# An attention-then-experts kernel: PSUM banks in another order, tokens transposed one pass ahead, r and k in one transfer

## The chip, the cores and the metric

The kernel runs on one core of a Trainium2 chip. The core has four compute engines with a queue of instructions each: TensorE (PE in the profile; its weight loads are shown as PEld), VectorE (DVE), ScalarE (ACT) and GpSimd (POOL). SyncE (SP) only starts DMA transfers here; POOL starts the indirect ones. Each engine works through its queue in the order of the program, and an instruction that waits holds up everything queued behind it. The metric is the device time of one execution in microseconds.

## The reference

Two blocks follow each other. The first is a linear attention with a decaying state, per batch `b` and head `h`:

```python
for t in range(S):
    cur = u[None] * k_t (outer) v_t
    y[:, :, t] = r_t @ (state + cur)
    state = w * state + k_t (outer) v_t
```

with 4 batches, 8 heads, 768 steps and head size 48. Its output, laid out as 3072 tokens of 384 numbers, goes into a mixture of 8 experts with one expert per token:

```python
logits = x @ w_gate                      # (3072, 8)
e = argmax(logits);  g = softmax(logits)[e]
out[token] = g * (relu(x @ w1[e]) @ w2[e])   # 384 -> 1024 -> 384
```

All inputs and outputs are float32.

## The kernel before

**Attention.** The 32 pairs of batch and head are worked off as 16 units of two heads (`U = 16`, four units per batch), one head in partitions 0 to 47, the other in 64 to 111. A unit is cut into `G = 6` chunks of 128 steps. Within a chunk the attention is a masked 128 x 128 score matrix; between chunks a 48 x 48 state is carried by a scan. The powers of the decay are put into r and k beforehand.

`load(i)` starts three transfers of unit `i` on SP: r and k of the first head into `rks`, r and k of the second head, and v and k in another layout into `vks`. `prep(i)` has three products: `RK`, r and k times the tables of decay (DVE, line 214), `rp`, r times k (POOL, line 217), and `Kd`, the keys with decay for the state (POOL, line 218). Then `p_own` multiplies `rp` by u on TensorE (line 227, the first TensorE work of a unit), `own_t` transposes that on DVE, `p_scores` makes the scores (line 239), `diag` writes u's diagonal on ACT (line 245), `mask` puts the scores above it (DVE), `p_ds` and `scan` make the states, `p_out` the output (lines 282 and 287), `p_tr` and `keep` turn it into token rows `xb` and add up the gate's logits. The loop over `i` is a pipeline written out by hand: unit `i` is scored, unit `i - 1` is put out, unit `i - 2` is transposed, unit `i + 1` is prepared, unit `i + 3` is loaded.

After every fourth unit `choose`, `p_rank` and `slots` find each token's expert and its place in it, and `send` scatters the token rows from `xb` to `rows` in DRAM by an indirect DMA on POOL (line 357), two chunks of 128 tokens in each of three units (three in each of two units for the third batch). `ids` (line 364), a POOL iota, writes the token numbers into `xb` for the next batch but one; it has to wait until the sends that read this `xb` are done. `clear` zeroes a part of `rows` (one large transfer, after unit 3). The weights of the first two experts are loaded in the same loop: `weights(0, 0)` and `weights(0, 1)` after units 6 and 9, expert 1's after units 13 and 14.

**Experts.** A pass is a stretch of an expert's tokens. Expert 0 has two passes (256 tokens, which stand before the last batch is routed, and 160), experts 1 to 6 one of 416 (`CAP`), the last expert two (160 and 256): ten passes. Per pass:

- `load` reads the token rows back into `xs` (four transfers, SP line 386);
- `xT` transposes them on DVE in three instructions (line 395);
- `L1` makes `hT`: for each of 8 groups `f` three matmuls into a bank of `hbank` (line 403), then a relu on ACT (line 405);
- `L2` makes the output: for each of 3 groups `m` eight matmuls into a bank of `ybank` (line 412), then a transpose on DVE (`yq`, line 414);
- `put` multiplies by the gate on DVE (`yo`, line 452) and scatters 32-token groups to the output with up to 13 indirect DMAs on POOL (line 455).

The last pass does its second layer the other way round, with tokens as the rows (`tokens_out`, lines 435 to 440), which leaves two scatters at the end. `xs` has three buffers, `xT`, `hT`, `yq` and `yo` two, the weights three.

The banks are two lists of PSUM tiles. `X23` and `yps` are each one tile of two banks:

```python
hbank = [X01[0], X01[1], X23[:, 0, :], X23[:, 1, :]]     # group f uses hbank[f % 4]
ybank = [yps[:, 0, :], yps[:, 1, :], dsb]                # group m uses ybank[m]
```

The order of the main loop is `xT(k)`, `L1(k)`, `L2(k-1)`, `load(k+1)`, `put(k-1)`, `weights`. TensorE therefore runs L1 of a pass, then L2 of the pass before it; on DVE `xT(k+1)` stands behind the three transposes of `L2(k-1)` and behind `put(k-1)`.

**The beginning.** SP's first transfers are, in order, the decay table `wt`, unit 0, `ubs` (u), unit 1, `wgs` (the gate's weights), unit 2. POOL builds an identity, masks and small tables of numbers (lines 107 to 135), the table `dec` for the scan (162, 163) and `sel`, the matrix by which `p_tr` transposes and multiplies by the gate at once (167, 168; the last of these instructions reads `wgs`). Only then comes `prep(0)`.

Behind the straight path stands a general one (`general`) for inputs that don't fit its bounds; with these inputs it is branched over.

Of the kernel before, what the change touches and what calls it, by code (L numbers as in the profile page):

```python
# [19 lines left out]
DM = H * D  # L20
# [20 lines left out]
def straight(tc, rk, vk, w, ub, wg, w1, w2, out, flag):  # L41
# [24 lines left out]
    hbank = [X01[0].rearrange("p a b -> p (a b)"), X01[1].rearrange("p a b -> p (a b)"), X23[:, 0, :], X23[:, 1, :]]  # L66
    ybank = [yps[:, 0, :], yps[:, 1, :], dsb]


    wt = cp.tile([KP, HP], FP32, name="wt")  # L70
    nc.sync.dma_start(wt, w)
    ubs = cp.tile([KP, HP, 2], FP32, name="ubs")
    wgs = cp.tile([KP, 2, HP, E], FP32, name="wgs")
# [7 lines left out]
    vks = [ca.tile([128, G, 2, 2 * D], FP32, name=f"vk{i}") for i in range(4)]  # L81

    def load(i):
        if i >= U:
            return
        b, hp = divmod(i, HP)
        n0 = 64 if i < 3 else D
        nc.sync.dma_start(rks[i % 3][0:n0], rk[b, hp, 0, 0:n0])
        nc.sync.dma_start(rks[i % 3][64:KP], rk[b, hp, 1, 0:D])
        nc.sync.dma_start(vks[i % 4], vk[b, hp])  # L90

    load(0)
    nc.sync.dma_start(ubs, ub)
    load(1)
    nc.sync.dma_start(wgs, wg)
    load(2)
# [10 lines left out]
    ident = cp.tile([128, 128], FP32, name="ident")  # L107
    make_identity(nc, ident)
# [4 lines left out]
    tri = cp.tile([128, 128], BF16, name="tri")  # L113
    ones = cp.tile([128, 128], BF16, name="ones")
    nc.gpsimd.tensor_copy(tri, strict)
    nc.gpsimd.memset(ones, 1.0)
    rev = cp.tile([128, E], FP32, name="rev")
    basef = cp.tile([128, E], FP32, name="basef")
    osum = cp.tile([128, E], BF16, name="osum")
    pos = cp.tile([128, CAP // 32], FP32, name="pos")  # L120
    pos2 = cp.tile([128, 4], FP32, name="pos2")
    it = cp.tile([128, 64], I32, name="it")
    nc.gpsimd.iota(it[:, 0:E], pattern=[[-1, E]], base=E, channel_multiplier=0)
    nc.gpsimd.tensor_copy(rev, it[:, 0:E])
    nc.gpsimd.iota(it[:, E:2 * E], pattern=[[N // 128, E]], base=0, channel_multiplier=0)
    nc.gpsimd.tensor_copy(osum, it[:, E:2 * E])
    nc.gpsimd.iota(it[:, 2 * E:3 * E], pattern=[[N, E]], base=0, channel_multiplier=0)
    nc.gpsimd.tensor_copy(basef, it[:, 2 * E:3 * E])
    ng = CAP // 32
    for a in range(4):  # L130
        q = slice(32 * a, 32 * a + 32)
        nc.gpsimd.iota(it[q, 32:32 + ng], pattern=[[32, ng]], base=0, channel_multiplier=1)
    nc.gpsimd.tensor_copy(pos, it[:, 32:32 + ng])
    nc.gpsimd.iota(it[:, 48:52], pattern=[[128, 4]], base=0, channel_multiplier=1)
    nc.gpsimd.tensor_copy(pos2, it[:, 48:52])

# [18 lines left out]
    for hp in range(HP):  # L155
        nc.tensor.transpose(tr[:, hp * 128:hp * 128 + KP], T3c[:, hp, :], ident[0:KP, 0:KP])
    T3 = cp.tile([128, HP, 2 * D], FP32, name="T3")
    nc.scalar.copy(T3.rearrange("p a (h d) -> p a h d", h=2),
                   tr.rearrange("p (a h d) -> p a h d", a=HP, h=2)[:, :, :, 0:D])

    dec = cp.tile([KP, HP, D, G - 1], FP32, name="dec")
    nc.gpsimd.memset(dec, 0.0)
    nc.gpsimd.tensor_copy(dec[:, :, :, 1:], bc(pw[:, 7, :, None, None], [KP, HP, D, G - 2]))
    for par in range(2):
        for h in range(2):
            o = 64 * (h ^ par)
            nc.gpsimd.tensor_copy(sel[:, par, :, h * D:(h + 1) * D], bc(ident[0:KP, None, o:o + D], [KP, HP, D]))
    nc.gpsimd.tensor_copy(sel[:, :, :, 2 * D:], wgs)
# [3 lines left out]
    nc.vector.tensor_scalar(out=le, in0=wt, scalar1=W_HI, scalar2=None, op0=ALU.is_le)  # L172
    nc.vector.scalar_tensor_tensor(out=okw, in0=wt, scalar=W_LO, in1=le, op0=ALU.is_ge, op1=ALU.mult)
# [35 lines left out]
    def prep(i):  # L209
        if i >= U:  # L210
            return
        hp = i % HP
        x, v = rks[i % 3], vks[i % 4]
        nc.vector.tensor_tensor(RKs[i % 3][0:KP].rearrange("p u (c t) -> p u c t", t=C),  # L214
                                x[0:KP].rearrange("p u (c t) -> p u c t", t=C),
                                bc(TT[:, hp, :, None, :], [KP, 2, G, C]), op=ALU.mult)
        nc.gpsimd.tensor_tensor(rps[i % 2][0:KP], x[0:KP, 0], x[0:KP, 1], op=ALU.mult)  # L217
        nc.gpsimd.tensor_tensor(Kds[i % 2], v[:, 0:G - 1, 1, :], bc(T3[:, hp, None, :], [128, G - 1, 2 * D]),  # L218
                                op=ALU.mult)
# [37 lines left out]
    def p_ds(i):  # L257
        v = vks[i % 4]
        d = dsb[:, 0:240].rearrange("p (e g) -> p e g", g=G - 1)
        for c in range(G - 1):  # L260
            for h in range(2):
                nc.tensor.matmul(d[64 * h:64 * h + D, :, c], lhsT=Kds[i % 2][:, c, h * D:(h + 1) * D],  # L262
                                 rhs=v[:, c, 0, h * D:(h + 1) * D], start=True, stop=True, skip_group_check=True)
# [7 lines left out]
    def p_out(i):  # L271
# [8 lines left out]
        for c in range(G):  # L280
            for h in range(2):
                nc.tensor.matmul(o(c, h), lhsT=v[:, c, 0, h * D:(h + 1) * D], rhs=A[:, place(c, h), :],  # L282
# [95 lines left out]
    class Pass:  # L378
# [28 lines left out]
        def L2(self, ms=range(DT)):  # L407
            y = self.y = yqs[self.k % len(yqs)]
            for m in ms:
                p = ybank[m]  # L410
                for f in range(FT):
                    nc.tensor.matmul(p[:, 0:self.n], lhsT=w2s[self.e % 3][:, f, m * 128:(m + 1) * 128],  # L412
                                     rhs=self.h[:, f, 0:self.n], start=f == 0, stop=f == FT - 1, skip_group_check=True)
                nc.vector.transpose(y[:, 0:self.g, 32 * m:32 * m + 32],  # L414
                                    p[:, 0:self.n].rearrange("p (g j) -> p g j", j=32))

        def load_ids(self):

            nt = self.n // 128
            nc.sync.dma_start(xg[:, 0:nt], rows[self.e * N + self.s0:self.e * N + self.s0 + self.n, 2 * D:Q].rearrange(  # L420
                "(t p) c -> p t c", p=128))

        def tokens_out(self):

            nt = self.n // 128
            nc.vector.tensor_scalar(out=vt[:, 0:nt], in0=pos2[:, 0:nt], scalar1=float(self.s0), scalar2=cnt[:, self.e:self.e + 1],
                                    op0=ALU.add, op1=ALU.is_lt)
            nc.vector.memset(it2, 1 << 20)
            nc.vector.tensor_scalar(out=ia[:, 0:nt], in0=xg[:, 0:nt, 1].bitcast(I32), scalar1=2, scalar2=None,
                                    op0=ALU.logical_shift_right)  # L430
            nc.vector.copy_predicated(it2[:, 0:nt], vt[:, 0:nt], ia[:, 0:nt])
            for t in range(nt):
                p = ybank[t]
                for f in range(FT):
                    nc.tensor.matmul(p[:, 0:DM], lhsT=self.h[:, f, t * 128:(t + 1) * 128], rhs=w2s[self.e % 3][:, f, :],  # L435
# [10 lines left out]
        def put(self):  # L446
            yo, ix, g = yos[self.k % len(yos)], ixs[self.k % 2], self.g
# [6 lines left out]
            for k in range(g):  # L454
# [7 lines left out]
    passes = [Pass(0, 0, EARLY, 0), Pass(0, EARLY, CAP - EARLY, 1)] + [Pass(e, 0, CAP, e + 1) for e in range(1, E - 1)] + \  # L462
             [Pass(E - 1, 0, LAST, E), Pass(E - 1, LAST, CAP - LAST, E + 1)]
# [3 lines left out]
    prep(0)  # L467
    for i in range(U + 1):
# [3 lines left out]
        if not last:  # L472
            p_own(i)
            own_t(i)
# [4 lines left out]
        prep(i + 1)  # L479
        if not last:  # L480
# [27 lines left out]
        if i == 3:  # L508
            clear()
        if i in (6, 9):  # L510
            weights(0, (i - 6) // 3)
        if i in (13, 14):
            weights(1, i - 13)
        if i == 14:
            count(cnt3)
            nc.vector.tensor_scalar(out=viol[:, 12:13], in0=cnt3[:, 0:1], scalar1=float(EARLY), scalar2=None, op0=ALU.is_lt)
        if i == U - 1:
            first.load()
    first.xT()
# [39 lines left out]
    first.L2()  # L559
    passes[1].xT()  # L560
    first.put()
    passes[1].L1()
    n = len(passes)
    for k in range(2, n):
        p = passes[k]
        if k == n - 1:
            passes[k - 1].L2()
            passes[k - 1].put()
        p.xT()
        p.L1()  # L570
        if k < n - 1:
            passes[k - 1].L2()
        if k + 1 < n:
            passes[k + 1].load()
        if k < n - 1:
            passes[k - 1].put()
            if 1 < p.e + 2 < E and p.e > 0:
                weights(p.e + 2)
# [10 lines left out]
def general(tc, rk, vk, w, ub, wg, w1, w2, out):  # L589
# [24 lines left out]
    nc.sync.dma_start(wu[0:D], w[0:D])  # L614
    nc.sync.dma_start(wu[64:KP], w[64:KP])
    wgs = consts.tile([128, HP, E], FP32, name="wgsg")
    nc.vector.memset(wgs, 0.0)
    nc.sync.dma_start(wgs[0:KP], wg[:, 0])
# [22 lines left out]
    nc.sync.dma_start(ubg[0:KP], ub)  # L641
# [65 lines left out]
    def load_pair(b, hp):  # L707
# [7 lines left out]
        nc.sync.dma_start(vt, vk[b, hp][:, :, 0, :])  # L715
# [320 lines left out]
def rwkv5_then_switch(tc, rk, vk, w, ub, wg, w1, w2, out):  # L1036
    nc = tc.nc
    with tc.tile_pool(name="fl", bufs=1) as fl:
        flag = fl.tile([1, 1], I32, name="flag")
        with tc.manual_schedule():  # L1040
            straight(tc, rk, vk, w, ub, wg, w1, w2, out, flag)
            bad = nc.values_load(flag[0:1, 0:1], engines=[ENG.PE, ENG.SP, ENG.DVE, ENG.Activation, ENG.Pool],
                                 min_val=0, max_val=E + HP + 1, skip_runtime_bounds_check_because="a sum of ones and zeros")
        with tc.If(bad > 0):
            general(tc, rk, vk, w, ub, wg, w1, w2, out)


def _layout(inputs):
# [8 lines left out]
    vk = _np.stack([a.reshape(B, HP, 2, G, C, D).transpose(0, 1, 4, 3, 2, 5).reshape(B, HP, C, G, 2 * D)  # L1057
                    for a in (v, k)], axis=4)
# [33 lines left out]
```

## Time and profile before

| | us |
|---|---|
| median of 3 runs (512.07 to 516.09) | 515.48 |
| the profiled execution, device time | 518.24 |
| its span, first to last instruction | 516.4 |
| TensorE busy in the span | 420.8 (81%) |
| GpSimd busy | 186.1 (36%) |
| VectorE busy | 152.5 (30%) |
| ScalarE busy | 113.8 (22%) |
| mean granted TensorE clock | 0.926 of full |
| first work of unit 0 on TensorE (L227) | at 17.6 |
| first L1 of the experts | at 158.1 |
| first L2 of the experts | at 172.1 |
| last TensorE instruction ends | at 509.2 |

All times inside the execution count from the first instruction of the span. In the rows that follow, a line number is that of the kernel before; a group such as `X<-xT,w1s` names the tile written and the tiles read; `x18` is the number of instructions merged into the row; what stands in brackets is how long the engine had been idle before the row and which engine and tile ended that wait. "issue" is idle time in which the profile shows nothing to wait for. Two records are shown for each float32 matmul. The profile's row of the clock has the clock that TensorE was granted, in tenths of full speed, in 40 slices of 12.9 us.

### The profile page before, as it was taken

What the parts mean: (1) busy time and instruction counts of PE and PEld (TensorE: products, weight loads), DVE (VectorE), ACT (ScalarE), POOL (GpSimd) and SP (SyncE); (2) the same over time, 40 slices, a digit from 0 to 9 for tenths busy, and PEclk for the clock granted to TensorE, in tenths of its full rate; (3) what the DMA queues carried; (4) which work ended last, traced back from release to release, by engine and by line L of the source; (5) the groups of instructions that cost most, each with busy time, mean ns of one, the idle gap of its engine ahead of it and who ended that gap; (6) DMA issues with size and microseconds to landing.
All of it is one profiled execution on the core that took longest, in us unless ns stands there. A gap on an engine that the chain in (4) does not pass through costs nothing.

```text
span 516.4 us, 6947 instructions
## 1 busy us (share of the span) xinstructions
PE 420.8 (81%) x2707; PEld 279.6 (54%) x2707; DVE 152.5 (30%) x327; ACT 113.8 (22%) x326; POOL 186.1 (36%) x189
## 2 busy tenths in 40 slices
PE   0498998789979889889978978979888996498394
PEld 0387786668758775644434434434444445347262
DVE  6488897477732130110020020030021002004000
ACT  1267666346622012011012002002101101000010
POOL 5764255488220441030054036027007205404711
PEclk9999999587969999989989989988998998699798
DMA  8947989666430396090092074037004002000100
GB/s 177 244 111 197 236 267 276 195 194 212 190 101 1 108 323 181 1 309 1 0 236 101 0 182 155 1 130 210 3 26 151 14 0 60 20 0 24 33 9 34
DMA packets 27129, 60.87 MB, mean 118 GB/s; under 512 B 17719, under 2 KB 18755, under 8 KB 25040
## 3 DMA queue, kind: packets, MB, share of 16 engines
q1 hardware_dynamic: 22352, 50.80, 34.8%
q0 software_dynamic: 4736, 9.55, 5.7%
q8 instruction: 23, 0.38, 0.3%
q14 instruction: 18, 0.15, 0.1%
HBM read 49.59 MB, written 11.13 MB: 118 GB/s over the span
## 4 chain that ended last, share of the span: by engine, by line
PE 72%; DVE 10%; issue 9%; ACT 3%; POOL 2%; another core or an unknown queue 1%; DMA 1%; DVEq 0%; POOLq 0%; ACTq 0%
PE X L403 30%; PE yps L412 16%; PE dsb L412 8%; PE X L239 4%; PE yps L282 4%; PE tr L300 3%; PE yps L435 2%; ACT hT L405 2%; DVE A L251 2%; PE yps L287 2%; DVE yo L452 2%; PE dsb L227 2%; ACT A L245 1%; PE dsb L262 1%
## 5 line engine op out<-in xcount | busy, mean ns | idle before, releaser
L403 PE MATMUL X<-xT,w1s 128*128 128x416 f32 (+2 forms) x480 | 156.4, 483 | 48.0 <-ACT hT L405 18.4
L455 POOL DMA_INDIRECT out_dram<-yo,ix x96 | 94.4, 983 | 221.6 <-DVE yo L452 121.6
L403 PEld LDWEIGHTS X<-xT,w1s 128*128 128x128 f32 x480 | 91.6, 207 | 111.3 <-issue 58.9
L405 ACT ACTIVATE hT<-X 128x416 f32<-128x416 f32 (+2 forms) x80 | 35.7, 448 | 301.3 <-PE X L403 226.3
L412 PE MATMUL yps<-hT,w2s 128*128 128x416 f32 (+2 forms) x288 | 88.1, 459 | 5.8 <-DVE yq L414 5.8
L414 DVE STREAM_TRANSPOSE yq<-yps 128x416 f32<-128x416 f32 (+2 forms) x18 | 9.7, 539 | 227.7 <-PE yps L412 222.1
L412 PEld LDWEIGHTS yps<-hT,w2s 128*128 128x128 f32 x288 | 51.7, 193 | 41.5 <-issue 30.1
L245 ACT ACTIVATE A<-ident,own 128x128 f32<-128x128 f32 x192 | 57.9, 388 | 25.1 <-DVE own L231 24.7
L357 POOL DMA_INDIRECT rows<-xb,slot x24 | 28.9, 1206 | 49.7 <-DVE osum L353 44.2
L412 PE MATMUL dsb<-hT,w2s 128*128 128x416 f32 (+2 forms) x144 | 42.8, 450 | 0.0
L214 DVE TENSOR_TENSOR RK<-rk,TT 112x1536 f32<-112x1536 f32 x16 | 38.1, 2378 | 0.0
L217 POOL TENSOR_TENSOR rp<-rk 112x768 f32<-112x768 f32 x16 | 32.1, 2008 | 13.7 <-PE X L239 6.5
L239 PE MATMUL X<-RK 48*128 48x128 f32 x384 | 35.7, 323 | 1.0 <-issue 1.0
L412 PEld LDWEIGHTS dsb<-hT,w2s 128*128 128x128 f32 x144 | 25.7, 190 | 15.7 <-issue 15.3
L239 PEld LDWEIGHTS X<-RK 48*128 48x128 f32 x384 | 28.6, 216 | 8.5 <-issue 7.5
L282 PE MATMUL yps<-A,vk 128*48 128x128 f32 x384 | 29.6, 309 | 1.5 <-issue 1.5
L282 PEld LDWEIGHTS yps<-A,vk 128*48 128x48 f32 x384 | 24.4, 141 | 4.7 <-issue 2.9
L227 PE MATMUL dsb<-rp,ubs 112*2 112x192 f32 x128 | 9.1, 358 | 20.1 <-POOL rp L217 13.6
L218 POOL TENSOR_TENSOR Kd<-vk,T 128x480 f32<-128x480 f32 x16 | 21.1, 1318 | 6.5 <-DMA vk<-in_vk_dram 3.7
L251 DVE COPY_PREDICATED A<-strict,X 128x512 f32<-128x512 int32 x32 | 22.2, 726 | 3.0 <-PE tr L300 1.8
L300 PE MATMUL tr<-sel,yT 112*128 112x104 f32 x128 | 20.7, 312 | 1.8 <-ACT A L245 1.2
L292 ACT COPY yT<-yps 112x384 f32<-112x384 f32 x32 | 13.8, 482 | 35.2 <-PE yps L287 30.9
(101 smaller groups left out, 228.9 us busy)
## 6 DMA issues: line engine op xcount, KB each, us to landing
w1s<-in_w_dram SPq DMA_DIRECT2D x8, 1536.0 KB
w2s<-in_w_dram SPq DMA_DIRECT2D x8, 1536.0 KB
vk<-in_vk_dram SPq DMA_DIRECT2D x16, 576.0 KB
rk<-in_rk_dram SPq DMA_DIRECT2D x29, 288.0 KB
xs<-rows SPq DMA_DIRECT2D x24, 159.2 KB
out_dram<-yo,ix POOLq DMA_INDIRECT x96
rows<-zt SPq DMA_DIRECT2D x1, 1176.0 KB
rk<-in_rk_dram SPq DMA_DIRECT2D x3, 384.0 KB
```

What stands on the lines that cost most here:

```text
L214: nc.vector.tensor_tensor(RKs[i % 3][0:KP].rearrange("p u (c t) -> p u c t", t=C), x[0:KP].rearrange("p u (c t) -> p u c t", t=C), bc(TT[: ...
L217: nc.gpsimd.tensor_tensor(rps[i % 2][0:KP], x[0:KP, 0], x[0:KP, 1], op=ALU.mult)
L239: nc.tensor.matmul(o, lhsT=r[q, 1, c * C:(c + 1) * C], rhs=r[q, 0, c * C:(c + 1) * C], start=True, stop=True, skip_group_check=True)
L245: nc.scalar.activation(A[:, place(c, h), :], ident, func=ACT.Copy, scale=own[i % 2][:, c, h:h + 1])
L251: nc.vector.copy_predicated(A[:, 4 * k:4 * k + 4, :], bc(m[:, None, :], [128, 4, C]), X01[k])
L282: nc.tensor.matmul(o(c, h), lhsT=v[:, c, 0, h * D:(h + 1) * D], rhs=A[:, place(c, h), :], start=c < 2, stop=c == 0, skip_group_check=True)
L300: nc.tensor.matmul(trv[c // 4][:, c % 4, :], lhsT=yTs[i % 3][0:KP, c & 1, (c // 2) * C:(c // 2 + 1) * C], rhs=sel[:, c & 1, i % HP, :], st ...
L357: s_ = nc.gpsimd.indirect_dma_start(out=rows[:, :], out_offset=bass.IndirectOffsetOnAxis(ap=slot[b % 2][:, c:c + 1], axis=0), in_=xbs[b % ...
L403: nc.tensor.matmul(p[:, 0:self.n], lhsT=w1s[self.e % 3][:, m, f * 128:(f + 1) * 128], rhs=self.t[:, m, 0:self.n], start=m == 0, stop=m == ...
L405: nc.scalar.activation(h[:, f, 0:self.n], p[:, 0:self.n], func=ACT.Relu)
L412: nc.tensor.matmul(p[:, 0:self.n], lhsT=w2s[self.e % 3][:, f, m * 128:(m + 1) * 128], rhs=self.h[:, f, 0:self.n], start=f == 0, stop=f == ...
L455: s_ = nc.gpsimd.indirect_dma_start(out=out4[:, :], out_offset=bass.IndirectOffsetOnAxis(ap=ix[:, k:k + 1], axis=0), in_=yo[:, k, :], in_o ...
```

## The change

- **Banks.** In `hbank` and `ybank` the two halves of the two-bank tiles no longer follow each other.
- **Tokens ahead.** `xT` of pass k+1 is issued right after L1 of pass k, ahead of L2 of pass k-1; the tokens are loaded two passes ahead.
- **The last expert.** It is one pass of 416 tokens: one L1, an L2 of its first 160 tokens, and `tokens_out` for the other 256. L2 of expert 6 now runs before L1 of expert 7. There are nine passes.
- **Loads.** r and k of both heads come in one transfer of 112 partitions, with the 16 padding rows between the heads. The k in `vks` has five chunks instead of six (the sixth isn't used). The decay table, u and the gate's weights are one array, `wug`, and come in one transfer ahead of everything.
- **Start.** `pairs(0)` (the product rp) comes ahead of the tables on POOL; `sel` is built after `prep(1)`, the tables of numbers after `prep(3)`; the transposes of the key table follow `p_own(0)` on TensorE. `prep` is split into `scale`, `pairs` and `keys`.
- **Later.** `clear` after unit 4 instead of 3; the weights of expert 0 after units 9 and 11 instead of 6 and 9; those of expert 1 after units 14 and 15 instead of 13 and 14.

```diff
-    hbank = [X01[0]..., X01[1]..., X23[:, 0, :], X23[:, 1, :]]
-    ybank = [yps[:, 0, :], yps[:, 1, :], dsb]
+    hbank = [X01[0]..., X23[:, 0, :], X01[1]..., X23[:, 1, :]]
+    ybank = [yps[:, 0, :], dsb, yps[:, 1, :]]
...
+    wug = cp.tile([KP, 3 * HP + 2 * HP * E], FP32, name="wug")
+    nc.sync.dma_start(wug, w)
...
-        nc.sync.dma_start(rks[i % 3][0:n0], rk[b, hp, 0, 0:n0])
-        nc.sync.dma_start(rks[i % 3][64:KP], rk[b, hp, 1, 0:D])
+        nc.sync.dma_start(rks[i % 3][0:KP], rk[b, hp].rearrange("h p u s -> (h p) u s")[0:KP])
...
-    prep(0)
+    pairs(0)
+    state_decay()
+    p_own(0)
+    own_t(0)
+    scale(0)
+    key_decay()
+    keys(0)
     for i in range(U + 1):
...
         if not last:
-            p_own(i)
-            own_t(i)
+            if i > 0:
+                p_own(i)
+                own_t(i)
             p_scores(i, range(4))
...
         prep(i + 1)
+        if i == 0:
+            selection()
+        if i == 2:
+            numbers()
...
-        if i == 3:
+        if i == 4:
             clear()
-        if i in (6, 9):
-            weights(0, (i - 6) // 3)
-        if i in (13, 14):
-            weights(1, i - 13)
+        if i in (9, 11):
+            weights(0, (i - 9) // 2)
         if i == 14:
+            weights(1, 0)
...
         if i == U - 1:
             first.load()
+            weights(1, 1)
...
-    first.L2()
+    first.L2(range(0, 2))
     passes[1].xT()
+    first.L2(range(2, 3))
+    passes[2].xT()
     first.put()
     passes[1].L1()
+    passes[3].load()
     n = len(passes)
-    for k in range(2, n):
-        p = passes[k]
-        if k == n - 1:
-            passes[k - 1].L2()
-            passes[k - 1].put()
-        p.xT()
-        p.L1()
-        if k < n - 1:
-            passes[k - 1].L2()
-        if k + 1 < n:
-            passes[k + 1].load()
-        if k < n - 1:
-            passes[k - 1].put()
-            if 1 < p.e + 2 < E and p.e > 0:
-                weights(p.e + 2)
+    for k in range(2, n - 1):
+        passes[k].L1()
+        passes[k + 1].xT()
+        passes[k - 1].L2()
+        passes[k - 1].put()
+        if k + 2 < n:
+            passes[k + 2].load()
+        if passes[k].e + 2 < E:
+            weights(passes[k].e + 2)
+    passes[-2].L2()
+    passes[-1].L1()
+    passes[-2].put()
+    passes[-1].L2(n=LAST)
+    passes[-1].put(LAST)
     passes[-1].tokens_out()
```

`state_decay` holds the two instructions for `dec`, `selection` those for `sel`, `numbers` the tables of numbers and two small DVE checks of w, `key_decay` the four transposes of the key table and their copy. Their instructions are those of before.

## The prediction

> **What bounds the kernel now.** I read the page first (engines, the 40 slices), then the timeline of TensorE through the experts, then the stretches where the chain of waits leaves TensorE: the start, the attention around 90 us, the last expert.
>
> ```profile
> PE 420.8 (81%) x2707; PEld 279.6 (54%) x2707; DVE 152.5 (30%) x327; ACT 113.8 (22%) x326; POOL 186.1 (36%) x189
> PEclk9999999587969999989989989988998998699798
> DMA  8947989666430396090092074037004002000100
> ```
>
> TensorE is the bound, but 81% busy flatters it: the clock row dips below 9 once or twice per expert. The DMA row is full only in the first 140 us. One expert and its neighbour, TensorE alone (start, length, operation, count, wait before it and who ended it):
>
> ```profile
> 289.26 5.85 PE L412 MATMUL yps<-hT,w2s 128*128 128x416 f32 x16 [0.71 <-DVE yq L414]
> 294.95 5.75 PE L412 MATMUL dsb<-hT,w2s 128*128 128x416 f32 x16
> 303.66 8.24 PE L403 MATMUL X<-xT,w1s 128*128 128x416 f32 x18 [2.96 <-DVE xT L395]
> 312.57 8.65 PE L403 MATMUL X<-xT,w1s 128*128 128x416 f32 x24 [0.67 <-ACT hT L405]
> 322.47 2.36 PE L403 MATMUL X<-xT,w1s 128*128 128x416 f32 x6 [1.25 <-ACT hT L405]
> ...
> 347.07 0.34 PEld L403 LDWEIGHTS X<-xT,w1s 128*128 128x128 f32 x1 [0.36 <-issue]
> 352.08 0.19 PEld L403 LDWEIGHTS X<-xT,w1s 128*128 128x128 f32 x1 [0.16 <-issue]
> ```
>
> Each matmul stands as two records, so an expert is 96. In dense stretches a record starts every 349 ns at 416 columns (216 ns at 256, 136 at 160, 323 for the 384-wide token products): 96 x 0.349 = 33.5 us. The cycle from 261.7 to 303.7 took 42.0, so 8.5 us are lost per expert: 2.96 for the transposed tokens (xT), 0.67 and again 0.67 to 1.34 where f=3 and f=7 wait for the relu of f=2 and f=6, 0.71 where m=1 waits for the transpose of m=0, a quarter of a microsecond of refill after each wait, and the clock: after the 2.96 us gap one or two stretches of 3.4 us run at half speed (the last two lines: 0.70 us per record, then 0.35), 1.7 to 3.4 us.
>
> **Experts: banks, tokens ahead.** f=2/f=3 and f=6/f=7 are the two halves of X23, m=0/m=1 the halves of yps; the wait falls exactly there, so it follows the tile and not the bank. In the new order a half meets its sister two groups later (4.2 us in L1, 5.6 us in L2), against 0.52 us of relu or 0.62 of transpose: those waits go. xT of the next pass moves on DVE's queue ahead of the three yq transposes and of put. It adds no instruction. Queued behind it are those transposes, and TensorE waits for them only at m=2 of L2. Its own input, xs, is now loaded two passes ahead: issued when put(k-1) has read its buffer, about 2.6 us into L1(k+1), and needed, if TensorE is not to notice, by m=2 of L2(k): 14.2 us rest of L1 + 11.2 us = 25 us later. The trace has an xs of 416 tokens issued until 182.0 and used at 186.1: at most 4.1 us. DVE has 5.1 us of work per expert, POOL 13 scatters x 1.29 = 16.8 us, a pair of weights 7.4 us of DMA: all below 33.5.
>
> Here a rule and a row part. The Trainium skill (TensorE: Matmul & The Clock Gate, Part 1) has the clock halve after a whole idle window of about 3.4 us. By that a 2.96 us gap costs itself alone, and closing all waits saves some 6 us per expert. The row shows half clock after gaps of 2.96 (and the expert loops at a mean of 0.93 to 0.96), so I take the full 8.5.
>
> **Last expert in one.** Before, L1 runs 48 records at 136 ns and 48 at 216: 16.9 us; in one at 416 columns 16.75: nothing by itself. But xT and the three yq transposes of the second part stood between (1.70 us wait), and two stalls lie here:
>
> ```profile
> 445.34 0.30 ACT L405 ACTIVATE hT<-X 128x160 f32<-128x160 f32 x1 [3.94 <-remote]
> ...
> 488.16 0.38 ACT L405 ACTIVATE hT<-X 128x256 f32<-128x256 f32 x1 [6.02 <-remote]
> 488.60 7.22 PE L403 MATMUL X<-xT,w1s 128*128 128x256 f32 x24 [8.57 <-issue]
> ```
>
> ACT gets TensorE's signals late while POOL issues scatters; the trace does not name the cause. TensorE then loses 7.7 and 8.6 us because f=3 depends on f=2. A wait of four groups (8.4 us at 416 columns) is the new cover. Ends: 0, or all 16.3 and the cold clock after them, 22. I take 6, nearer 0, since in the 416-wide passes the same lateness was at most 1.4 us.
>
> Dense sum from the first L2 on: 48 x 0.216 + 144 x 0.136 + (7 + 6) x 48 x 0.349 + 32 x 0.323 = 10.4 + 19.6 + 217.8 + 10.3 = 258.1 us, where before it took 172.1 to 509.2 = 337.1. Added back: 1.7 us, because xT(1) cannot start before its xs has landed (178.2 first issue, so TensorE still waits between L2(0) and L1(1), where it waited 1.08), and the 6 above. **MoE: 266.**
>
> **The start.**
>
> ```profile
> 15.57 0.24 POOL L168 COPY sel<-wgs 112x64 f32<-112x64 f32 x1 [7.05 <-DMA wgs<-in_wg_dram]
> 15.77 1.80 POOL L217 TENSOR_TENSOR rp<-rk 112x768 f32<-112x768 f32 x1
> 17.63 0.82 PE L227 MATMUL dsb<-rp,ubs 112*2 112x192 f32 x8 [8.19 <-POOL rp L217]
> ...
> 24.66 0.82 PE L227 MATMUL dsb<-rp,ubs 112*2 112x192 f32 x8 [2.08 <-DVE S L267]
> ```
>
> POOL stands 7 us on the gate weights, which lie behind two units of loads, and rp(0) behind it. After: the small tables (34 KB) come first, then rk0, 688 KB. From 3 to 27 us the trace moved 5.55 MB, 0.231 MB/us; 2.56 MB had passed when wgs was there, so transfers count from about 3.9 us. rk0 lands at 7.0, vk0 9.4, rk1 12.3, vk1 14.7. rp(0) 7.0 to 8.8, dec (2 x 0.89) to 10.6, own scores 8.8 to 10.0 with the transpose, RK(0) to 11.8, T3's four transposes and copy to 11.1, Kd(0) to 12.3, scores to 13.9, p_ds and the rest (1.0 + 1.2) to 16.1, mask and scan to 17.4. Unit 1 then begins at 17.5 instead of 24.66: **7.2 us**. selection (2.3 us) lands on POOL in unit 0's tail and numbers (2.6 us) in unit 2, where POOL has 3 to 4.7 of 7 us: hidden.
>
> rk in one transfer carries 112 rows instead of 96, vk 11 blocks instead of 12: per unit 1.23 MB for 1.18, at 0.231 MB/us 5.3 us against a unit of 6.6 to 7.3: hidden while nothing else is queued. One SP issue of 0.4 us less per unit is off the path.
>
> **Weights later.**
>
> ```profile
> 91.44 0.19 POOL L364 IOTA xb<- 128x24 int32 x1 [6.52 <-DMA vk<-in_vk_dram]
> ...
> 93.48 0.82 PE L227 MATMUL dsb<-rp,ubs 112*2 112x192 f32 x8 [5.39 <-POOL rp L217]
> ...
> 122.50 0.19 POOL L364 IOTA xb<- 128x24 int32 x1 [1.93 <-DMA rows<-xb,slot]
> ```
>
> At unit 8 POOL's iota rewrites xb and waits for the sends that read it; rp(10), so TensorE, stands behind. The sends took 6.4 us to land beside the w1 load (DMA share 1.0), 1.8 us at unit 12 with DMA idle. Then half clock to 105.7. From unit 9 to the first L1 (81.5 to 158.1) 76.6 us went where 51 would do (six units of 6.7 and 11 of tail). Now w1 leaves at unit 9 and w2 at 11, so unit 8 is relieved but unit 12 loaded, between units 9 and 12 by 1.57 MB more than before, 3.7 us. The skill (DMA: Bandwidth & Descriptors, Arbitration) has each engine take its queues in turn, packet by packet: a send beside any busy queue would wait about double, 3.6 us, and moving weights would gain nothing, for the loads keep that queue busy at unit 8 too. The row says 6.4 beside weights and 1.8 without. Ends: 1 us lost against before, 18 gained. I take 4, nearer the rule: the stall moves more than it goes.
>
> **The sum.** First L2 begins at 172.1 - 7.2 - 4 - 0.9 (two bank waits of 0.47 in the first L1) = 160.0. Plus 265.8, and 7.2 us from TensorE's end to the span's end as before: 433.0. The profiled execution took 518.24 for a span of 516.4, 1.8 more: 434.8. The median shown, 515.48, is 0.5% lower: **433**.
>
> **Rivals.**
> 1. *The stall is only moved.* Attention gains the start alone, late signals cost 22 again: 167 + 258.1 + 1.7 + 22 + 9 = 458. For: their cause is unnamed, and DMA is full. Against: four banks of cover.
> 2. *Everything opens.* No stall of sends, no late signals: 146 + 259 + 9 = 414. Against: DMA at share 1.0 between 46 and 95 us.
> 3. *The banks do nothing* (the waits follow something else): 2 us plus refill in eight passes, 433 + 18 = 451. Against: f=3, f=7 and m=1 alone wait.
> 4. *Slower: xs in front of DVE.* xT(k+1) stands ahead of L2(k-1)'s transposes; an xs later than its 25 us of slack holds DVE, then both yps banks, six times. To lose the 85 us gained it must land 25 + 14 = 39 us after issue; the row has 4.1 at most. A chance only if scatters and weights starve it.
>
> **How the numbers follow.** Forecast 0.62 (420 to 446), rival 1 0.15, rival 3 0.08, rival 2 0.10, slower 0.03, about equal 0.02. The range 416 to 458 takes in the unknowns' ends and leaves out a tenth to two. A measurement of this kernel tells about 1% from no change: faster 0.95, same 0.02, slower 0.03.
>
> **What would show it.** First own scores near 9 us and unit 1 near 17.5. L403 and L412 in unbroken runs of 48 records, no "<-DVE xT" and no "<-ACT hT" of 0.67, clock 9 or more from slice 13 on, expert cycles of 33.5 us. iota at unit 8 waiting under 4 us, at unit 12 about 5. It is wrong if expert cycles stay above 37, or if waits on DVE xT appear in L1.

## The result, and the profile after

The changed kernel took **441.2 us** (median of four runs, 438.47 to 447.05) against 515.7 for the kernel before in the same round: a ratio of 0.855, with an interval of 0.849 to 0.862. (A ratio leaves out runs more than 1.5% above the fastest of their kernel, here that of 447.05; a median does not.) It is faster, as forecast, and 8 us above the predicted 433. The profiled execution took 438.47 for a span of 436.7. These rows of its page stand against the first three shown of before:

```profile
PE 396.9 (91%) x2659; PEld 265.6 (61%) x2659; DVE 152.1 (35%) x324; ACT 112.2 (26%) x318; POOL 189.0 (43%) x189
PEclk9999999867798999999999999999999999998997
DMA  8947787848713417913701900900910920001001
```

TensorE is now busy for 91% of the span. The clock stays at 9 or above through the whole expert loop (a slice is now 10.9 us) and dips in the attention (slices 7 to 12, counted from 0) and at the end. The other engines have the same work as before in a shorter span.

TensorE's timeline through one expert and into the next, columns as in the prediction:

```profile
201.68 16.92 PE L417 MATMUL X<-xT,w1s 128*128 128x416 f32 x48
218.44 5.75 PE L428 MATMUL yps<-hT,w2s 128*128 128x416 f32 x16
224.03 5.75 PE L428 MATMUL dsb<-hT,w2s 128*128 128x416 f32 x16
229.62 5.75 PE L428 MATMUL yps<-hT,w2s 128*128 128x416 f32 x16
235.20 16.92 PE L417 MATMUL X<-xT,w1s 128*128 128x416 f32 x48
```

The 48 records of L1 stand in one row, and no row ends in a bracket: TensorE waits for nothing. The cycle is 235.20 - 201.68 = 33.52 us, 96 records of 0.349, where it was 42. In the stretch from 235.2 (busy time of TensorE, its weight loads, DVE, ACT, POOL; then clock, DMA share and GB/s) TensorE is busy for all 33.50 us at full clock:

```profile
235.20:268.70 33.50, 33.50 (x97) 18.24 (x96) 5.13 (x10) 4.14 (x8) 12.77 (x13) 1.00 0.39 129
387.00:411.70 24.70, 18.96 (x49) 9.67 (x48) 2.30 (x5) 3.51 (x7) 14.00 (x15) 0.93 0.08 26
```

The second row is the last expert's L1, where 48 records take 24.7 us instead of 16.9. Its timeline, with the second layer ahead of it:

```profile
370.15 5.85 PE L428 MATMUL yps<-hT,w2s 128*128 128x416 f32 x16 [0.71 <-DVE yq L430]
375.85 5.75 PE L428 MATMUL dsb<-hT,w2s 128*128 128x416 f32 x16
381.43 5.75 PE L428 MATMUL yps<-hT,w2s 128*128 128x416 f32 x16
387.02 10.64 PE L417 MATMUL X<-xT,w1s 128*128 128x416 f32 x30
401.05 6.15 PE L417 MATMUL X<-xT,w1s 128*128 128x416 f32 x12 [3.39 <-issue]
409.55 2.36 PE L417 MATMUL X<-xT,w1s 128*128 128x416 f32 x6 [2.35 <-ACT hT L419]
```

Five of the eight groups run (6 records each), then TensorE stands for 3.39 us and, two groups later, for 2.35; between the two the clock is halved for 3.4 us. ACT shows why: its relus should come every 2.09 us, and come late, most with "remote" (a source that the profile cannot name) as what they waited for:

```profile
389.38 0.52 ACT L419 ACTIVATE hT<-X 128x416 f32<-128x416 f32 x1 [33.21 <-PE X L417]
392.00 0.52 ACT L419 ACTIVATE hT<-X 128x416 f32<-128x416 f32 x1 [2.11 <-issue]
395.55 0.52 ACT L419 ACTIVATE hT<-X 128x416 f32<-128x416 f32 x1 [3.03 <-remote]
400.48 0.52 ACT L419 ACTIVATE hT<-X 128x416 f32<-128x416 f32 x1 [4.41 <-remote]
404.73 0.52 ACT L419 ACTIVATE hT<-X 128x416 f32<-128x416 f32 x1 [3.74 <-remote]
```

The relu at 400.48 is that of f=3; it ends at 401.00, and TensorE goes on with f=5 at 401.05. f=3 and f=5 are the two halves of `X23`.

The beginning:

```profile
6.88 2.35 POOL L228 TENSOR_TENSOR rp<-rk 112x768 f32<-112x768 f32 x1 [4.99 <-DVE TT L123]
9.28 0.82 PE L241 MATMUL dsb<-rp,wug 112*2 112x192 f32 x8 [9.28 <-POOL rp L228]
18.35 0.82 PE L241 MATMUL dsb<-rp,wug 112*2 112x192 f32 x8 [1.52 <-DVE S L281]
```

and POOL's iotas ahead of the products rp of units 10 and 14, which had waited 6.52 and 1.93 us:

```profile
82.34 0.19 POOL L378 IOTA xb<- 128x24 int32 x1 [4.10 <-DMA rows<-xb,slot]
115.63 0.19 POOL L378 IOTA xb<- 128x24 int32 x1 [4.21 <-PE yps L296]
```

The profile names the sends for the first wait and TensorE for the second. TensorE stood 2.94 us for rp at the start of unit 10 and not at all for it at unit 14.

Of 79.7 us of span, 68.3 came between the first L2 and TensorE's end (337.1 to 268.8). That divides into 7.3 up to the first layer of expert 2, 33.5 in four steady expert cycles, and 27.5 from expert 6's first layer on. Of these 27.5 some 7.9 are expert 6's own cycle; the rest, the last expert's part, is read from the two traces alone, for no run puts its second pass back. The start gave 6.3, the attention and first L1 the rest.

### The profile page after: what moved, and what is told of

It is laid out like the page before. It is cut to its first block, busy times and chain, and to the rows that moved or that the text cites. A ratio compares the mean times of both kernels' runs of the same rounds, so it can differ in the third digit from the quotient of the medians.

```text
span 436.7 us, 6777 instructions
## 1 busy us (share of the span) xinstructions
PE 396.9 (91%) x2659; PEld 265.6 (61%) x2659; DVE 152.1 (35%) x324; ACT 112.2 (26%) x318; POOL 189.0 (43%) x189
## 4 chain that ended last, share of the span: by engine, by line
PE 76%; DVE 7%; issue 4%; another core or an unknown queue 3%; POOL 3%; ACT 2%; DMA 2%; POOLq 0%; DVEq 0%; ACTq 0%
PE X L417 28%; PE yps L428 19%; PE dsb L428 9%; PE X L253 5%; PE yps L296 4%; PE tr L314 3%; PE dsb L241 2%; PE dsb L276 2%; PE yps L301 2%; ACT A L259 2%; POOL rp L228 1%; DMA rows<-xb,slot 1%; DVE RK L222 1%; PE yps L447 1%
## 5 line engine op out<-in xcount | busy, mean ns | idle before, releaser
L417 PE MATMUL X<-xT,w1s 128*128 128x416 f32 (+2 forms) x432 | 138.4, 479 | 6.9 <-issue 3.4
L417 PEld LDWEIGHTS X<-xT,w1s 128*128 128x128 f32 x432 | 79.6, 192 | 63.2 <-issue 57.1
L419 ACT ACTIVATE hT<-X 128x416 f32<-128x416 f32 (+2 forms) x72 | 34.3, 478 | 227.6 <-PE X L417 189.5
L428 PE MATMUL yps<-hT,w2s 128*128 128x416 f32 (+2 forms) x288 | 85.8, 451 | 0.7 <-DVE yq L430 0.7
L253 PE MATMUL X<-RK 48*128 48x128 f32 x384 | 36.7, 328 | 2.3 <-DVE RK L222 1.6
L409 DVE STREAM_TRANSPOSE xT<-xs 128x416 f32<-128x416 f32 (+2 forms) x27 | 13.1, 535 | 46.6 <-DMA xs<-rows 46.6
L241 PE MATMUL dsb<-rp,wug 112*2 112x192 f32 x128 | 9.4, 369 | 18.1 <-POOL rp L228 12.2
L232 POOL TENSOR_TENSOR Kd<-vk,T 128x480 f32<-128x480 f32 x16 | 23.3, 1458 | 3.4 <-PE dsb L276 2.8
```

What stands on the lines that cost most here:

```text
L232: nc.gpsimd.tensor_tensor(Kds[i % 2], v[:, G:2 * G - 1, :], bc(T3[:, hp, None, :], [128, G - 1, 2 * D]), op=ALU.mult)
L253: nc.tensor.matmul(o, lhsT=r[q, 1, c * C:(c + 1) * C], rhs=r[q, 0, c * C:(c + 1) * C], start=True, stop=True, skip_group_check=True)
L417: nc.tensor.matmul(p[:, 0:self.n], lhsT=w1s[self.e % 3][:, m, f * 128:(f + 1) * 128], rhs=self.t[:, m, 0:self.n], start=m == 0, stop=m == ...
L419: nc.scalar.activation(h[:, f, 0:self.n], p[:, 0:self.n], func=ACT.Relu)
L428: nc.tensor.matmul(p[:, 0:n], lhsT=w2s[self.e % 3][:, f, m * 128:(m + 1) * 128], rhs=self.h[:, f, 0:n], start=f == 0, stop=f == FT - 1, sk ...
```

## The experiments

Each is told with its edit against the changed kernel unless it says otherwise. Times are medians; a ratio is to the kernel before in the same round.

### The three causes in the expert loop

**Banks back in the old order.**

```diff
-    hbank = [X01[0]..., X23[:, 0, :], X01[1]..., X23[:, 1, :]]
-    ybank = [yps[:, 0, :], dsb, yps[:, 1, :]]
+    hbank = [X01[0]..., X01[1]..., X23[:, 0, :], X23[:, 1, :]]
+    ybank = [yps[:, 0, :], yps[:, 1, :], dsb]
```

> The changed kernel with the old order of hbank and ybank. Theory (waits follow the two-bank tile): 0.67 + 0.67 + 0.71 us and a quarter of refill after each come back per pass, 2.8 us, over some seven passes 18 us; the late signals of the last expert are exposed more, up to 8. 455 to 468. Rival (the waits had another cause and the banks do nothing): 441, with expert cycles still at 33.5 us.

460.4 us (458.6 to 461.9), ratio 0.894 [0.887, 0.902]. TensorE's timeline in one expert:

```profile
244.38 6.45 PE L417 MATMUL X<-xT,w1s 128*128 128x416 f32 x18
251.49 8.65 PE L417 MATMUL X<-xT,w1s 128*128 128x416 f32 x24 [0.67 <-ACT hT L419]
260.81 2.36 PE L417 MATMUL X<-xT,w1s 128*128 128x416 f32 x6 [0.67 <-issue]
...
269.46 5.86 PE L428 MATMUL yps<-hT,w2s 128*128 128x416 f32 x16 [0.71 <-DVE yq L430]
```

The three waits are back at the places where they stood before, after 18, 42 and 16 records. A cycle is 36.36 us, 2.84 more: 2.05 of waiting and a refill of a quarter of a microsecond behind each. The clock in the loop stays full. The dependency follows the tile, as the prediction had it.

**The transpose back behind put.** `passes[k + 1].xT()` stands after `passes[k - 1].put()` again; loads stay two passes ahead.

> The changed kernel with the next pass's xT behind put on DVE, as before the change (loads still two passes ahead). Theory (gap plus half clock): 2.96 us, refill and 1.7 to 3.4 us of clock come back per expert, 5 to 6.5 us in six experts: 470 to 480, and the clock row dips once per expert. Rival ([...]the gap costs itself alone): 3.2 us per expert, 460, clock 1.00.

460.1 us (459.5 to 463.7), ratio 0.897 [0.889, 0.905]. Two experts of TensorE's timeline:

```profile
243.39 18.54 PE L417 MATMUL X<-xT,w1s 128*128 128x416 f32 x48 [2.95 <-DVE xT L409]
...
281.65 17.03 PE L417 MATMUL X<-xT,w1s 128*128 128x416 f32 x48 [2.96 <-DVE xT L409]
```

The gap is as long as before, but only the first of the two L1 that follow it takes 18.54 us instead of 16.9. Cycles alternate: 36.74 and 38.3. So the gap costs 3.2 us in itself, and one stretch of half clock (3.4 us at half speed, 1.5 us lost) behind two of the four gaps of this length. The expectation of 470 to 480, which put the half clock behind every gap, missed. The rival's 460 came out, though not its clock of 1.00.

**The new banks alone**, in the kernel before (the same two lines, nothing else changed).

> The kernel before with the new order of hbank and ybank alone. Theory (parts add up): 2.8 us per expert, eight passes, 20 us less than before, 495. Rival (short waits and the gap together keep the clock low, so each removed alone brings more or less than its own time): L1 after the gap may get its clock back sooner, 485 to 490, or the dips stay at one per expert, 495 to 500.

493.2 us (491.3 to 500.3), ratio 0.950 [0.938, 0.963]. The first five of its expert cycles took 36.5 to 39.7 us, a mean of 37.9, which is 3.9 less than the 41.8 of before. That is more than the 2.84 that the same edit is worth in the loop without gaps. The rest is the clock, which in the kernel before dips in every expert and here only in some. Here three of the four gaps of 2.96 us have half clock behind them. So 33.52 + 2.84 + 3.2 = 39.6 of the 41.8 are the work and the two kinds of waits, and the last 2.2 are half clock, which the gap alone brings behind some gaps and the bank waits alone not at all.

### The last expert's late signals

**Without expert 6's scatters.** The 13 scatters of expert 6 are left out, and with them its rows of the output.

> The changed kernel without the thirteen scatters of expert 6 (its rows of the output stay unwritten), so that POOL issues nothing while L1 of the last expert runs. Theory (the late signals come from POOL's scatters): L1 of the last expert takes 16.9 us instead of 24.7, total some 8 us less, 433. Rival (they come with the place in the program, for example from SP's state): still 24.7.

433.87 us in one run (span 431.8). The last L1 in TensorE's timeline, and a stretch of ACT's:

```profile
389.30 16.92 PE L417 MATMUL X<-xT,w1s 128*128 128x416 f32 x48
```

```profile
400.04 0.52 ACT L419 ACTIVATE hT<-X 128x416 f32<-128x416 f32 x1 [1.58 <-PE X L417]
402.13 0.52 ACT L419 ACTIVATE hT<-X 128x416 f32<-128x416 f32 x1 [1.58 <-PE X L417]
```

From the second on the relus come every 2.09 us, and L1 is dense. Only the first, at 392.98, is 1.3 us late; the scatters of expert 5 had ended at 390.8. POOL's scatters are what delays the signals.

**SP held.** An unused load of weights is queued on SP so that SP waits for TensorE through the last expert, as it does in the loop:

```diff
     passes[-2].L2()
     passes[-1].L1()
+    nc.sync.dma_start(w1s[passes[-1].e % 3], w1[0])
     passes[-2].put()
```

> The changed kernel with one more load of weights on SP (w1 of expert 0, into the buffer that the last L1 reads), which keeps SP waiting for TensorE until the last L1 is over, as it waits in the loop, and not at the kernel's end. Scatters stay. Theory (late signals need SP in its wait for the scatters at the end): L1 of the last expert 16.9 us, total 433. Rival (scatters alone make them): 24.7, total 441.

442.7 us in one run. The last L1 takes 24.9 us, and the relus are as late:

```profile
405.94 0.52 ACT L419 ACTIVATE hT<-X 128x416 f32<-128x416 f32 x1 [4.47 <-remote]
411.58 0.52 ACT L419 ACTIVATE hT<-X 128x416 f32<-128x416 f32 x1 [5.12 <-PE X L417]
```

What SP does is not the cause.

**Without expert 5's scatters.** In the changed kernel two second layers follow each other without a first layer between them, and POOL works off expert 5's and expert 6's scatters as one run of 26, from 372.1 to 406.3, with one pause of 1.3 us. Here the 13 of expert 5 are left out (its rows of the output with them); expert 6's stay beside the last L1.

> Leaves out the 13 scatters of expert 5 (its rows of the output are not written); expert 6's 13 stand as in the changed kernel, but begin with no run ahead of them. Theory A (signals get late only behind a long run, 20 or so scatters one right after the other, or when the earlier run still fills the queue): the last first layer takes 17 to 19 us, 432 to 435 us. Theory B (13 scatters beside the last first layer are enough): 24 to 25 us, 440 to 442 us.

433.31 us in one run (span 431.4). The run of 13 lies from 390.9 to 407.3, beside the last L1 (TensorE) from 2.8 us after its start on, and the relus (ACT) keep their step:

```profile
388.06 16.92 PE L417 MATMUL X<-xT,w1s 128*128 128x416 f32 x48
```

```profile
400.89 0.52 ACT L419 ACTIVATE hT<-X 128x416 f32<-128x416 f32 x1 [1.58 <-issue]
402.98 0.52 ACT L419 ACTIVATE hT<-X 128x416 f32<-128x416 f32 x1 [1.58 <-PE X L417]
```

So it is not scatters beside L1 as such: the same 13 leave this L1 dense when no run stands ahead of them, as theory A of the expectation has it. But a run of 13 alone can delay signals too. The next one, from the first group of the second layer, whose products ended at 407.16, reached DVE at 409.48 and cost TensorE 0.56 us. And in the changed kernel's loop the last relu of expert 6's first layer, due at 352.8 beside a run of 13, came 2.9 us late, where TensorE did not wait for it:

```profile
355.65 0.52 ACT L419 ACTIVATE hT<-X 128x416 f32<-128x416 f32 x1 [4.43 <-remote]
```

**Fewer scatters.** Expert 6 is ended as expert 7 is, with 5 + 2 scatters in place of 13, queued ahead of the last L1:

```diff
...
-    passes[-2].L2()
+    passes[-2].L2((1, 2, 0), n=LAST)
+    passes[-2].put(LAST)
+    passes[-2].tokens_out()
     passes[-1].L1()
-    passes[-2].put()
```

The lines left out give expert 6 its own tiles for this ending and load its token numbers.

> Expert 6 is ended as expert 7 is: its second layer gives 160 tokens in the feature order and 256 in the token order, with 5 + 2 scatters in place of 13, and its scatters are queued ahead of the last expert's first layer. Theory (GpSimd's run of scatters makes TensorE's signals late): the run beside the last first layer is 7 long at most and ends some 8 us earlier, the last first layer takes 17 to 20 us in place of 24.7, and the 0.71 us wait between the two second layers that follow each other goes or moves: 433 to 437 us. Rival: any scatter beside the last first layer makes its signals late, however few: 440 to 443 us, as the changed kernel.

445.1 us (444.5 to 445.9), ratio 0.861 [0.856, 0.866]: no gain, 4 us more than the changed kernel by the medians, and above both forecasts. POOL's run is now 20 long, from 374.6 to 402.1. The last L1 begins at 390.07. Its first relu, due at 392.4, comes at 402.45 (ACT), and DVE reads a token product that was done at 390.23 only at 400.22:

```profile
402.45 0.52 ACT L419 ACTIVATE hT<-X 128x416 f32<-128x416 f32 x1 [43.01 <-remote]
400.22 0.62 DVE L452 TENSOR_SCALAR yt<-dsb,xg 128x384 f32<-128x384 f32 x1 [12.86 <-remote]
```

Both are 10 us late. DVE's own signal to POOL in this stretch is not: its product ended at 400.84 and the scatter that uses it began at 401.12. In the changed kernel's last L1, too, ACT's signal to TensorE took 0.05 us (401.00 to 401.05). So what TensorE sends is late, whichever of the two engines waits for it.

TensorE waits after three groups, for f=3 is the other half of f=1's tile:

```profile
390.07 6.45 PE L417 MATMUL X<-xT,w1s 128*128 128x416 f32 x18
403.78 12.67 PE L417 MATMUL X<-xT,w1s 128*128 128x416 f32 x30 [7.27 <-ACT hT L419]
```

A run of 20 is still too long. The lesson of the pair, for matmuls of 416 columns: the delay belongs to the later part of a run of scatters, not to their number beside L1.

### The start and the weights

**The old beginning.** The tables are built ahead of `prep(0)`, and the gate's weights load behind unit 1, as before.

> The changed kernel with the old beginning: decay, u and gate weights in three loads between the units, POOL's tables and sel ahead of rp(0). Theory (rp(0) stands behind the gate weights): unit 1 at 24.6 instead of 18.3 us, total 6 to 7 us more, 447 to 449. Rival (the attention is bound by transfers further on, so an early start is given back): 441 to 443.

444.6 us (441.3 to 447.1), ratio 0.862 [0.855, 0.870]. That is between the two forecasts. Against 441.2 the medians differ by 3.4 us, and the intervals overlap. The trace is clearer (first matmuls of units 0 and 1 on TensorE):

```profile
15.78 0.82 PE L244 MATMUL dsb<-rp,wug 112*2 112x192 f32 x8 [6.35 <-POOL rp L231]
...
22.81 0.82 PE L244 MATMUL dsb<-rp,wug 112*2 112x192 f32 x8 [2.07 <-DVE S L284]
```

Unit 1 begins at 22.81; in the eleven profiles with the new beginning it does so between 17.1 and 18.8. The start is worth 4 to 6 us where it happens.

**r and k in two transfers.**

```diff
-        nc.sync.dma_start(rks[i % 3][0:KP], rk[b, hp].rearrange(...)[0:KP])
+        n0 = 64 if i < 3 else D
+        nc.sync.dma_start(rks[i % 3][0:n0], rk[b, hp, 0, 0:n0])
+        nc.sync.dma_start(rks[i % 3][64:KP], rk[b, hp, 1, 0:D])
```

> The changed kernel with r and k of a unit in two transfers as before (64 and 48 rows in the first three units, 96 and 48 later). Theory: the transfers are off the path once the first three are in, so it is the same within 1 per cent (439 to 444 us); the first may land up to 1 us earlier or later. Rival: the two transfers a unit cost as much as the prediction gave to the whole start, 446 to 449 us.

443.3 us (439.8 to 447.4), ratio 0.852 [0.845, 0.859]. No difference that can be told: the single transfer is not where the time came from.

**Weights and clear at the old units** (3, 6, 9, 13, 14).

> The changed kernel with the old times of clear and weights (units 3, 6, 9, 13, 14). Theory of the prediction (the stall moves more than it goes): 4 us more, 445. Rival A (spreading the weights is worth all of it): 455 to 459. Rival B (the iota waits for sends beside any busy queue, weights or not): within 1 of 441.

440.3 us (438.9 to 443.0), ratio 0.855 [0.848, 0.862], the same. POOL's two iotas:

```profile
83.73 0.19 POOL L378 IOTA xb<- 128x24 int32 x1 [4.99 <-DMA rows<-xb,slot]
114.72 0.19 POOL L378 IOTA xb<- 128x24 int32 x1 [1.92 <-DMA rows<-xb,slot]
```

6.9 us of waiting instead of 8.3: moving the loads moves the wait from one unit to the other. It is worth nothing.

**The iota two units later**, when its sends have landed.

```diff
-        if i % 4 == 0 and i < U:
+        if i % 4 == 2 and i < U:
```

> The changed kernel with the token numbers written after units 2, 6, 10 and 14 instead of 0, 4, 8 and 12, so that the iota comes when the sends that read this buffer have landed. Theory (the iota's wait of 4.1 and 4.2 us and the half clock after it are what is left in the attention): no wait before the iota, units 9 to 13 at some 7 us each, first L1 10 to 15 us earlier, 427 to 432. Rival (transfers bound this stretch): the wait moves to the loads of r, k and v, 438 to 441.

442.2 us (439.2 to 445.0), ratio 0.851 [0.842, 0.860]. Both waits are gone and nothing is gained; neither theory had the reason. POOL no longer pauses there, so it runs the products of two units one after the other (from 77.7 to 83.6), and DVE meets them:

```profile
80.63 3.07 DVE L333 TENSOR_TENSOR sub<-lg,mx 128x48 f32<-128x48 f32 x1
```

In the changed kernel that subtraction of 48 numbers per partition took 0.21 us in three places and 0.58 in a fourth. It stands in the chain that routes the tokens, unit 10 takes 12.4 us, and the clock halves all the same (between its slices 7 and 12 the clock row falls to 6).

**TensorE kept busy.** Six added matmuls run on TensorE ahead of units 10 and 14 (4.1 us each time), so that its clock is not halved there; their result is not used.

```diff
+            if i in (10, 14):
+                for _ in range(6):
+                    nc.tensor.matmul(X01[0]..., lhsT=ident, rhs=T3..., start=True, stop=True)
```

> The changed kernel with six added matmuls (128 x 384, float32, 0.65 us each, 3.9 us in sum, their result unused) ahead of the first matmul of units 10 and 14, where TensorE waits for GpSimd's row numbers. Theory (what the two waits cost is the half clock that follows them, 10.2 us each): no half clock at 84 and 104 us, units 9 to 12 take 7 to 8 us in place of 10 to 11.5, and the first layer of the experts begins at 138 to 143 in place of 147: 431 to 437 us. Rival (the units wait for the engines' chain, the clock only follows): no gain, or up to 4 us more, 441 to 446 us.

438.0 us (433.3 to 444.8, five runs). The ratio, from three of the five, is 0.839 [0.832, 0.845], below the changed kernel's interval; by the medians of all runs the gain is 3 us. The profile is of the slowest of the five. In it units 10 to 12 take 7.7, 6.6 and 6.6 us at full clock where they took 11.5, 9.8 and 10.7, which is what the theory says of the first wait. But the second iota then waits twice as long:

```profile
81.06 0.19 POOL L378 IOTA xb<- 128x24 int32 x1 [4.03 <-DMA rows<-xb,slot]
117.33 0.19 POOL L378 IOTA xb<- 128x24 int32 x1 [8.84 <-DMA rows<-xb,slot]
```

The units came sooner, their sends with them, and these now share the DMA engines with weights: from 110 to 115 us the loads on SP's queue (packets, MB, share of 16 engines) moved 1.50 MB, in the changed kernel 0.77.

```profile
q1 hardware_dynamic: 157, 1.50, 72.7%
```

Unit 14 stands behind that iota through rp on POOL. The half clock came back behind that wait, and the first L1 began at 151.4 in this profile. Whether the version is better by 1 to 2% is not settled. That the half clock is a real part of the attention's cost is: units 10 to 12 took 20.8 us without it and 32.0 with it.

## Why the prediction was right, and where it was not

**Banks and tokens ahead: right.** 33.5 was forecast for a cycle and 33.52 measured, no wait on xT or on a bank is left in the loop, and the clock row holds from slice 13 to the last expert. In this sum the row was weighed against the clock rule (the Trainium skill, TensorE: Matmul & The Clock Gate, Part 1: half clock after a whole idle window of about 3.4 us). The total of 8.5 us per expert was right (8.3 measured), and the reading behind it half so: gaps of 2.96 us alone, shorter than the rule asks, were followed by half clock in two of four cases and in three of four, not always and not never. That it came in every expert before needed the bank waits as well.

**xs ahead: right.** DVE waits for its tokens up to 9.3 us, and TensorE waits for none of it; rival 4 did not come near its 39 us.

**The last expert: the mechanism right, two terms short.** 6 us were allowed for late signals; it was 8.0 (24.7 for 16.75). That the choice fell so near within a range of 0 to 22 was in part luck: it rested on signals that were late by at most 1.4 us in the 416-wide passes, and here the relu of f=4, due at 397.8, came 7.0 us late. The cover was mis-sized: "a wait of four groups (8.4 us)" holds only for the two single banks. For f=3, f=5 and f=7, which lie in `X23`, it is the two groups to the sister half, 4.2 us, by the tile rule that the prediction itself had used a part earlier; both waits in the last L1 stand there. Nor did the prediction see that L2 of expert 6 ahead of L1 of expert 7 joins two runs of scatters into one of 26, or that the last group of one L2 and the first of the next are the two halves of `yps`: 0.71 us at 370.15, and 0.44 at the token products for the same reason. The 1.7 us for xT(1) was 0.5. Together the part from the first L2 to TensorE's end took 268.8 against 265.8 forecast.

**The start: 6.3 of 7.2 us.** Unit 1 began at 18.35 and not at 17.5. rp(0) took 2.35 us instead of 1.80, beside DVE's work on its tables, and the two halves of RK(0) took 4.76 us, at 2.4 each, instead of 1.75 each. The durations of a later unit were carried to a place with other neighbours.

**Weights later: the number came out by luck, its reason fell.** From unit 9 to the first L1 the profile shows 72.5 us for 76.6, the 4 that was forecast. But undoing the move changed nothing, and seven profiles with this part of the program unchanged give 72.5 to 76.4 there, a mean of 75.2: the profiled execution was the shortest of them, and against the mean the gain is 1.4. The rule that spoke against this part (the Trainium skill, DMA: Bandwidth & Descriptors, Queues, rings and completion order: a queue's packets take turns with any other busy queue's) was right with its zero, within what these runs can tell. The waits came out at 4.10 and 4.21 us, where "under 4" and "about 5" were forecast.

**From span to median.** The prediction took 0.5% off because the profiled run of before lay above its median. The profiled run of after lies 0.6% below its own, so that step had the wrong sign. The 8.2 us between 433 and 441.2 are 3.7 of span (0.9 start, 3.0 experts, the rest small terms that nearly cancel) and 4.5 from this step, 1.8 taken off where 2.7 belonged on.

**Rivals.** 3 (banks do nothing) is refuted by two runs. 1 was right in that the sends' stall only moves, and wrong by 14 us on the last expert. 2 needed both stalls gone.

**What stays open.** Why a long run of scatters holds back TensorE's signals was not settled. Length is not the whole of it: in the kernel before, a run of 13 alone (429.6 to 446.0) beside the 160-column L1 made signals up to 7 us late (the products of f=6 ended at 438.0, their relu began at 445.34), and in the changed kernel's last L1 a run of 13 alone did not. There TensorE's records came 136 ns apart and here 349; whether that matters was not tried. Four separate tiles for the four banks of L1 (a cover of 8.4 us throughout), spacing the 26 scatters, or putting a first layer between the two second layers again, were not tried; by the two runs with 13 scatters fewer, on-time signals are worth some 8 us.

## What to carry to other kernels

Dependencies follow the tile, so two banks in one tile are one buffer with two halves: put the other buffers between them, and look at the seams between loops too. When several kinds of small waits stand in a loop, what each is worth can depend on the others through the clock; undo them one at a time from the fast end and do one alone from the slow end, and look at the clock where the two differ. Before believing a stage's gain of a few microseconds, compare that stage in several profiles in which it is the same program.

## What was not expected of the hardware

- Signals from TensorE, to ACT and to DVE, were up to 10 us late in the later part of POOL's back-to-back scatters (20 or 26 in a run at 1.29 us each). A run of 13 alone left the relus of the same L1 on time and made the next signal 2.3 us late; beside 160-column matmuls 13 were enough for 7 us. With 13 scatters left out, and none late enough to hold the last L1, the kernel takes 433 to 434 us.
- A DVE subtraction that takes 0.21 us took 3.07 while POOL ran two products back to back; it ended at 83.70, POOL's run at 83.63. The one of 0.58 us in the changed kernel ended at 123.29, a product on POOL at 123.23. The Trainium skill (SBUF — State Buffer, SBUF: two separate sides) says that DVE and GpSimd share a pair of ports that one of them holds for a whole instruction; the ends, 0.06 and 0.07 us apart, agree with that. That the wait of 3.07 us spans two products (from 80.66 and from 82.43) and not one does not follow from it and stays open. This is the price of a free POOL.
- A gap of 2.95 us in TensorE's work, repeated every 37 to 40 us, was followed by half clock in two of four cases in one kernel (3.4 us each) and in three of four in another.
